# Second batch's attention in the paired form of the later batches, from step 10

## The chip, the cores and the metric

The kernel runs on one core of a Trainium2 chip. The metric is the device time of one execution in microseconds (us), as the median of several runs; beside it stands one profiled execution, from which every trace row here is taken. TensorE (PE in the rows, its weight loads PEld) multiplies matrices, VectorE (DVE), ScalarE (ACT) and GpSimd (POOL) work element by element, SyncE (SP) issues the transfers.

## The reference

Eight batches of causal attention with a window of 128 keys and a linear bias by head, and behind it, over all 4608 tokens, a two-layer network with the mish activation. Cut to what matters:

```python
# q, k, v: batch 8, heads 8, tokens 576, head size 64
scores = q @ k.T / 8 + slope[h] * -(i - j)       # where 0 <= i - j < 128, else -1e9
attn = softmax(scores);  attn_out = attn @ v
x = attn_out.transpose(0, 2, 1, 3).reshape(4608, 512)
h = x @ w_in                                     # 512 -> 2048
g = h * tanh(softplus(h))                        # mish
out = g @ w_out                                  # 2048 -> 512
```

## The kernel before

**Stages.** Tokens go through the network in chunks: chunk c holds the first 512 tokens of batch c (the last 64 of all batches make up a ninth chunk, kept in DRAM in the meantime). Every chunk has a first layer (tiles h, 192 matmuls of 128x512, then mish on ScalarE into g) and a second layer (tiles po, output products). Values are split into a high and a low part, so that each product is three matmuls (gg is g in its two parts, si and so are the weights in theirs). A second layer has 32 steps: 16 weight blocks, each with two banks po0 and po1 and six matmuls a step ("a group of six"); after eight blocks a half of the chunk is complete and its two banks are copied out (ob), the first by VectorE, the second by ScalarE, before the next half may write a bank again.

**Attention beside it.** While chunk c is in its second layer, the attention of batch c+1 is placed between its groups. Heads go in pairs p = 0..3; a pair has two halves of 256 queries (`unit(b, p, half)`, eight of them in a batch) and the last 64 queries (`last_unit(b, p)`). A unit's steps are: `scores` (TensorE, into bank s), `exps(0)` and `exps(1)` (VectorE adds the bias and takes the maximum, tt-reduce into pz; ScalarE takes the exponential and its sum sm), `fold` (adds the two parts of the wrapped window; for the second batch on GpSimd, later on VectorE), `scale` (by 1/sm; for the second batch GpSimd, later VectorE and ScalarE), `weights` (TensorE transposes pz into the score bank, VectorE copies back and multiplies by masks), `values` (TensorE, value products into bank o for the first half and into bank pt_pl for the second), `late_half` (the value products of 64 rows each, `late_values`) and `split_x` (the result in two parts as input of the next first layer). The last queries have their own tiles pz_pl, pt_pl and pf_pl; pt_pl is also the bank of the second half's values.

**What sets the order.** Each step has a time in units (lists `times` in `unit` and `last_unit`); `attention(b)` adds the unit's number and sorts; the loop over chunks maps a unit time s to a place among the 32 steps by `begin + (n - 2.1 - begin) / units * s` with n = 32 and sorts once more. TensorE's and SyncE's instructions then stay in that order. Those of VectorE, ScalarE and GpSimd are put in order when the program is built, except where `in_order` fixes them; each engine executes its own queue strictly in order.

**The second batch is special.** Chunk 0's second layer starts inside the hand-written opening (`FIRST_STEPS`), which does groups up to the fifth block and ends with the conversion of the weights; so only 22 of the 32 steps are left for the second batch's attention, where later batches have all 32. Before the change it has its own times: half 1's scores a unit after half 0's, the late products of half 0 apart from those of half 1, and `begin, units = 11.5, 9.0` with a `lead` for the first two units.

Of the kernel before, what the change touches and what calls it, by code (L numbers as in the profile page):

```python
# [68 lines left out]
def attention_mish_mlp(  # L69
# [85 lines left out]
    def load(dst, src):  # L155
        sp.dma_start(out=dst, in_=src)
# [140 lines left out]
    def load_pair(b, p):  # L297
        t = at.tile([P, QKZ], F32, tag="qk", name=f"qk{b}_{p}")
        load(t, qk_[b, p])
        qkv[(b, p)] = parts_of(t)  # L300

    def load_v(b, p):

        pl, tag = (xp, f"x{p}") if p < NP - 1 else (at, "v")
        t = pl.tile([P, 2, 4, P], F32, tag=tag, name=f"v{b}_{p}", bufs=1)
        load(t, v[b, p])
        if b:
            load(vb[p % 2], vl_[b, p])
        qkv[("v", b, p)] = ((t[:, 0], t[:, 1]), vb[p % 2])

    def score_banks(name):
        return ps.tile([P, 2, 512], F32, tag="s", name=f"s{name}", bufs=2)
# [27 lines left out]
    def late_values(b, p):  # L340
        parts = late.pop((b, p))
        for n in range(max(len(part) for part in parts)):
            for i in range(2):
                for part in parts:
                    if n < len(part):
                        o, val, w = part[n](i)
                        pe.matmul(o, lhsT=val, rhs=w, start=False, stop=n == len(part) - 1, skip_group_check=True)

    def unit(b, p, half):
# [122 lines left out]
                        part(b, p, o, 256 * u)  # L472

        def late_half():
            if b == 1 or half == 1:
                late_values(b, p)

        times = (0, 0.02, 0.25, 0.7, 0.95, 1.3, 1.99, 2.02, 1.9995)
        if b > 1:

            times = (
                (-1, -0.8, -0.7, -0.57, -0.25, 0.7 if p == 1 else 0.65, 0.97, 0.996, 0.995) if half
                else (0, 0.02, 0.12, 0.4, 0.45, 1.4 if p == 1 else 1.3, 1.96, 1.96, 1.96)
            )
        return list(zip(times, (
            scores, lambda: exps(0), lambda: exps(1), fold, scale, weights, values, split_x, late_half,
        )))

    def last_unit(b, p):

        st = {}
        name = f"{b}_{p}l"

        def scores():
            _, keys, z = qkv[(b, p)]

            t = qkv[("s", b, p)] = score_banks(f"{b}_{p}_0")
            st["s"] = t[:, :, :96]
            for a in range(2):
                for r in HEAD:  # L500
                    pe.matmul(
                        st["s"][r, a, :], lhsT=z[:, r], rhs=keys(slice(0, P), 384 + 96 * a, 96),
                        start=True, stop=True, skip_group_check=True,
                    )

        def exps():
            mx = at.tile([P, 1], F32, tag="mxl", name=f"mx{name}")
            sm = st["sm"] = at.tile([P, 1], F32, tag="sml", name=f"sm{name}")
            pz = st["pz"] = at.tile([P, 192], F32, tag="pzl", name=f"pz{name}")
            dve.tensor_tensor_reduce(  # L510
                out=pz.rearrange("p (a n) -> p a n", a=2), in0=st["s"],
                in1=nl[:, p, :].rearrange("p (a n) -> p a n", a=2), scale=-SCALE, scalar=3.0e38,
                op0=ALU.add, op1=ALU.min, accum_out=mx,
            )
            act.activation(pz, pz, AF.Exp, bias=mx, scale=-1.0, accum_out=sm)

        def fold():
            sm, pz = st["sm"], st["pz"]
            act.activation(sm, sm, AF.Copy, bias=1e-9)
            dve.reciprocal(sm, sm)  # L520
            un = at.tile([P, 1], F32, tag="unl", name=f"un{name}", bufs=1)
            dve.tensor_tensor_reduce(
                out=pz[:, :64], in0=pz[:, :64], in1=pz[:, P:], scale=sm, scalar=3.0e38,
                op0=ALU.add, op1=ALU.min, accum_out=un,
            )
            act.activation(pz[:, 64:P], pz[:, 64:P], AF.Copy, scale=sm)

        def weights():
            t = st["t"] = qkv[("t", b, p)] = ps.tile([P, 512], F32, tag="w", name=f"pt{name}")
            pe.transpose(t[:, :P], st["pz"][:, :P], ident)  # L530
            pf = st["pf"] = at.tile([P, 2, 2, 64], F32, tag="pfl", name=f"pf{name}", bufs=1)
            shape = [P, 2, 2, 64]
            dve.tensor_tensor(
                out=pf, in0=t[:, :P].rearrange("p (u i n) -> p u i n", u=1, i=2).to_broadcast(shape),
                in1=masks[:, :2, :64].rearrange("p u (i n) -> p u i n", i=1).to_broadcast(shape),
                op=ALU.mult,
            )

        def values():
            va, vl = qkv[("v", b, p)]  # L540
            o = st["o"] = qkv[("ol", b, p)][:, 256 : 256 + LEFT]
            for i in range(2):
                pe.matmul(
                    o[HEAD[i]], lhsT=va[0][:, 3, HEAD[i]], rhs=st["pf"][:, 0, i, :],
                    start=False, stop=False, skip_group_check=True,
                )
            late[(b, p)][0].append(lambda i: (o[HEAD[i]], vl[:, HEAD[i]], st["pf"][:64, 1, i, :]))

        def keep():
            o = st["o"]  # L550
            xo = at.tile([P, LEFT], F32, tag="xo", name=f"xo{name}", bufs=5)
            dve.tensor_copy(xo, o)
            sp.dma_start(out=xs[p, :, b * LEFT : (b + 1) * LEFT], in_=xo)

        times = (-0.001, 0.5, 0.9, 1.4, 1.995, 1.9996)
        if b > 1:
            times = (-0.035, 0.21, 0.44, 1.78 if p == 1 else 1.7, 1.98, 1.9955)
        return list(zip(times, (scores, exps, fold, weights, values, keep)))

    def first_attention():  # L560
# [181 lines left out]
    def attention(b):  # L742

        steps = []
        for k in range(2 * NP):
            p, half = divmod(k, 2)

            lead = (0.7, 0.35)[k] if b == 1 and k < 2 else 0
            work = unit(b, p, half)
            if b == 1 and k < 2:

                for n in ((3,), (1, 2))[k]:
                    work[n] = (work[n][0], lambda f=work[n][1]: in_order(f))
            steps += [(k + d - (lead if n < 5 else 0), f) for n, (d, f) in enumerate(work)]
            if half == 0:
                steps += [(k + d - (lead if n < 3 else 0), f) for n, (d, f) in enumerate(last_unit(b, p))]
            if half:  # L760
                nxt = (b, p + 2) if p + 2 < NP else (b + 1, p + 2 - NP)
                if 0 < nxt[0] < B:
                    steps.append((k + 0.03, lambda nxt=nxt: load_pair(*nxt)))
                if b and p < 2:
                    steps.append((k + (1.0 if b > 1 else 2.01), lambda p=p: load_v(b, p + 2)))
        return sorted(steps, key=lambda s: s[0])

    def last_x():
# [30 lines left out]
    def mish(c, j):  # L799
        f = 2 * (j % 2)  # L800
        act.activation(gt[(c, j // 2)][:, f : f + 2, :], hs.pop((c, j)), AF.Mish)
# [3 lines left out]
    def parts(c, half, j):  # L805
        parts_high(c, half, j)
        parts_low(c, half, j)
# [59 lines left out]
    def in_order(work):  # L867
        dve.fixed = act.fixed = True
        work()
        dve.fixed = act.fixed = False  # L870
# [29 lines left out]
    steps = first_attention()  # L900
# [30 lines left out]
    for c in range(B + 1):  # L931
        for j in range(NJ if c else 0):
            if j == NJ - 1:
                parts(c, 0, 0)
                parts(c, 0, 1)
            first(c, j)
            mish(c, j)

        n = 4 * NJ
        steps = []  # L940
        if 0 < c < B - 1:
            steps += [(-0.5, lambda p=p: load_v(c + 1, p)) for p in range(2)]
        for m in range(2 * NJ):
            if c or f"U{m}" not in done:
                for t in range(2):
                    steps.append((2 * m + t, lambda m=m, t=t: second(c, *divmod(m, NJ), t)))
            if m >= 2 and (c or f"R{m}" not in done):
                steps.append((2 * m - 4.1, lambda m=m: parts(c, *divmod(m, NJ))))
        if c + 1 < B:
            begin, units = (1.4, 8.0) if c else (11.5, 9.0)  # L950
            steps += [(begin + (n - 2.1 - begin) / units * s, f) for s, f in attention(c + 1)]
        elif c + 1 == B:
            steps.append((4.5, last_x))
        for _, work in sorted(steps, key=lambda s: s[0]):
            work()
# [85 lines left out]
```

## Time and profile before

| | us |
|---|---|
| median of 3 runs (965.27 to 966.36) | 966.11 |
| profiled execution | 965.23 |
| its span in the trace | 963.5 |
| TensorE busy | 955.9 |
| ScalarE busy | 459.5 |
| VectorE busy | 351.5 |
| GpSimd busy | 257.3 |

The profiled execution lasts 1.7 us longer than its span, which counts from the first to the last instruction. Busy is the union of an engine's instructions; since matmuls are pipelined, a busy TensorE still has a start-to-start distance that depends on what follows what, so stretches are compared from start to start here. "idle before, <-" in a row is the time in which the engine waited and the engine that ended it.

### The profile page before, as it was taken

The page shows a single profiled execution, that of the slowest core. Times are in us where ns is not written, and L with a number is a line of the kernel's source. Part 1 is how long each engine was busy: PE and PEld are TensorE (multiplying, and loading weights), DVE is VectorE, ACT ScalarE, POOL GpSimd, SP SyncE. Part 2 cuts the span into 40 slices and gives each one's busy share as a digit, 9 for nine tenths or more (in the row PEclk, how much of TensorE's full clock was granted, in tenths as well). Part 3 has the DMA queues.
Part 4 walks back from the last instruction along what each step waited for, and adds up shares of the span by engine and source line. Part 5 has one row for each costly group of instructions (what it writes and reads, how often), then busy time and mean ns, then how long its engine had stood idle before and what let it go on. Part 6 is the DMA issues. An engine that isn't in the chain of part 4 may idle for free.

```text
span 963.5 us, 17830 instructions
## 1 busy us (share of the span) xinstructions
PE 955.9 (99%) x6868; PEld 781.3 (81%) x6868; DVE 351.5 (36%) x1456; ACT 459.5 (48%) x1290; POOL 257.3 (27%) x228
## 2 busy tenths in 40 slices
PE   9999999999999999999999999999999999999998
PEld 7788778888888888888888888888888888888886
DVE  6998660067203650166204640166005730100000
ACT  7997642276425752376225742466316642322121
POOL 5588541022112221032102311032102311241042
PEclk9999999999999999999999999999999999999999
DMA  9962320123002310122002310222003110000001
GB/s 345 395 245 90 109 78 22 41 86 105 24 1 74 127 48 6 54 84 93 24 1 95 107 54 1 74 79 77 24 23 105 50 46 1 22 22 22 1 15 29
DMA packets 29636, 69.83 MB, mean 72 GB/s; under 512 B 7408, under 2 KB 9712, under 8 KB 29552
## 3 DMA queue, kind: packets, MB, share of 16 engines
q1 hardware_dynamic: 29552, 68.69, 20.6%
q8 instruction: 54, 0.88, 0.4%
q14 instruction: 30, 0.25, 0.1%
HBM read 58.20 MB, written 10.49 MB: 71 GB/s over the span
## 4 chain that ended last, share of the span: by engine, by line
PE 88%; DMA 5%; DVE 4%; ACT 2%; issue 1%; SPq 0%; DVEq 0%; ACTq 0%
PE po L57 39%; PE h L57 36%; PE s L57 7%; PE o L57 3%; DMA wi<-in_moe_w_in_dram 2%; DVE to L57 1%; DMA wo<-in_moe_w_out_dram 1%; DMA v<-in_v_dram 1%; DVE pz L57 1%; PE pt_3l L57 1%; PE pt_2l L57 1%; PE pt_1l L57 1%; PE pt_0l L57 1%; DMA first<-in_tabs_dram 0%; DVE wo L57 0%
## 5 line engine op out<-in xcount | busy, mean ns | idle before, releaser
L57 PE MATMUL po<-so,gg 128*128 128x512 f32 x1728 | 420.8, 396 | 0.0
L57 PE MATMUL h<-x,si 128*128 128x512 f32 x1728 | 393.8, 389 | 0.0
L57 PEld LDWEIGHTS h<-x,si 128*128 128x128 f32 x1728 | 324.1, 188 | 67.4
L57 PEld LDWEIGHTS po<-so,gg 128*128 128x128 f32 x1728 | 317.1, 188 | 71.7 <-issue 8.9
L57 POOL TENSOR_TENSOR gg<-g,gg 128x512 fp32r<-128x512 f32 x144 | 186.2, 1296 | 650.0 <-ACT gg L57 647.2
L57 ACT ACTIVATE g<-h 128x1024 f32<-128x1024 f32 x72 | 74.1, 1029 | 257.0 <-PE h L57 255.3
L57 DVE CUSTOM_DVE_ANT_0 pz<-s,nb 64x128 f32<-64x128 f32 (+1 forms) x280 | 83.1, 327 | 292.4 <-PE s L57 289.9
L57 ACT ACTIVATE pz<-pz,mx 128x192 f32<-128x192 f32 (+1 forms) x256 | 110.8, 434 | 39.0 <-DVE mx L57 37.0
L57 ACT ACTIVATE gg<-g 128x512 fp32r<-128x512 f32 x144 | 90.0, 625 | 69.6 <-PE po L57 67.3
L57 PE MATMUL s<-qk 64*64 64x192 f32 (+2 forms) x1120 | 56.6, 300 | 0.0
L57 DVE CUSTOM_DVE_ANT_0 pz<-pz,sm 128x64 f32<-128x64 f32 x144 | 55.9, 436 | 1.3
L57 DVE COPY ob<-po 128x512 f32<-128x512 f32 x10 | 6.9, 692 | 128.1 <-PE po L57 128.1
L57 ACT ACTIVATE pz<-pz,sm 128x128 f32<-128x128 f32 (+1 forms) x192 | 53.2, 347 | 0.1
L57 DVE TENSOR_TENSOR pz<-s,masks 128x512 f32<-128x512 f32 (+1 forms) x56 | 51.5, 945 | 2.6 <-PE s L57 2.6
L57 ACT ACTIVATION_READ_ACCUMULATOR pz<-pz,mx 128x1 f32 x256 | 47.8, 187 | 0.0
L57 PEld LDWEIGHTS s<-qk 64*64 64x64 f32 (+1 forms) x1120 | 42.5, 134 | 3.9 <-issue 2.8
L57 PE MATMUL s<-ident,pz 128*128 128x128 f32 (+1 forms) x280 | 42.9, 275 | 0.4 <-POOL pz L57 0.3
L57 PEld LDWEIGHTS o<-pz,v 128*64 128x64 f32 (+1 forms) x656 | 30.2, 135 | 15.5 <-DVE pz L57 5.4
L57 PEld LDWEIGHTS s<-ident,pz 128*128 128x128 f32 (+1 forms) x280 | 34.5, 138 | 10.1 <-POOL pz L57 1.1
L57 PE MATMUL o<-pz,v 64*64 64x64 f32 (+3 forms) x656 | 40.5, 250 | 0.4 <-DVE pz L57 0.4
L57 ACT ACTIVATE ob<-po 128x512 f32<-128x512 f32 x26 | 15.6, 599 | 44.1 <-PE po L57 44.1
L57 DVE DVE_READ_ACCUMULATOR2_ANT mx<- 128x1 f32 (+1 forms) x312 | 25.3, 81 | 0.0
(172 smaller groups left out, 551.8 us busy)
## 6 DMA issues: line engine op xcount, KB each, us to landing
qk<-in_qk_dram SPq DMA_DIRECT2D x28, 640.0 KB, 4.3
v<-in_v_dram SPq DMA_DIRECT2D x32, 512.0 KB, 4.3
wi<-in_moe_w_in_dram SPq DMA_DIRECT2D x16, 512.0 KB, 10.5
wo<-in_moe_w_out_dram SPq DMA_DIRECT2D x16, 512.0 KB, 10.2
out_dram<-ob SPq DMA_DIRECT2D x32, 256.0 KB, 2.0
first<-in_qk_dram SPq DMA_DIRECT2D x2, 848.0 KB, 9.6
xr<-xs SPq DMA_DIRECT2D x4, 256.0 KB, 2.7
out_dram<-ob SPq DMA_DIRECT2D x8, 128.0 KB, 2.4
```

Of the source, the lines that this page charges most:

```text
L57: ins = method(*args, **kwargs)
```

## The change

The second batch gets the times of the third and later batches: half 1's scores directly behind half 0's, weights of half 1 shortly behind those of half 0, late products of both halves together (`late_half` acts in half 1 alone). `lead` and the `in_order` marks of the first two units are gone, the loads of v come at unit time 1.0, and the attention begins at step 10 with 8 units over the rest. `fold` and `scale` stay on GpSimd for the second batch.

```diff
         def late_half():
-            if b == 1 or half == 1:
+            if half == 1:
                 late_values(b, p)
...
-        times = (0, 0.02, 0.25, 0.7, 0.95, 1.3, 1.99, 2.02, 1.9995)
-        if b > 1:
-
-            times = (
-                (-1, -0.8, -0.7, -0.57, -0.25, 0.7 if p == 1 else 0.65, 0.97, 0.996, 0.995) if half
-                else (0, 0.02, 0.12, 0.4, 0.45, 1.4 if p == 1 else 1.3, 1.96, 1.96, 1.96)
-            )
+        times = (
+            (-1, -0.8, -0.7, -0.57, -0.25, 0.7 if p == 1 else 0.65, 0.97, 0.996, 0.995) if half
+            else (0, 0.02, 0.12, 0.4, 0.45, 1.4 if p == 1 else 1.3, 1.96, 1.96, 1.96)
+        )
...
-        times = (-0.001, 0.5, 0.9, 1.4, 1.995, 1.9996)
-        if b > 1:
-            times = (-0.035, 0.21, 0.44, 1.78 if p == 1 else 1.7, 1.98, 1.9955)
+        times = (-0.035, 0.21, 0.44, 1.78 if p == 1 else 1.7, 1.98, 1.9955)
...
-            lead = (0.7, 0.35)[k] if b == 1 and k < 2 else 0
-            work = unit(b, p, half)
-            if b == 1 and k < 2:
-
-                for n in ((3,), (1, 2))[k]:
-                    work[n] = (work[n][0], lambda f=work[n][1]: in_order(f))
-            steps += [(k + d - (lead if n < 5 else 0), f) for n, (d, f) in enumerate(work)]
+            steps += [(k + d, f) for d, f in unit(b, p, half)]
...
-                    steps.append((k + (1.0 if b > 1 else 2.01), lambda p=p: load_v(b, p + 2)))
+                    steps.append((k + 1.0, lambda p=p: load_v(b, p + 2)))
...
-            begin, units = (1.4, 8.0) if c else (11.5, 9.0)
+            begin, units = (1.4, 8.0) if c else (10.0, 8.0)
```

How it moves instructions, at three places. Names carry batch, pair and half: s1_0_1 and pz1_0_1 are batch 1, pair 0, half 1; pt1_0l is the last queries' bank of pair 0; po0_0_1 is chunk 0, half 0, bank 1; an operand "ident" marks a transpose.

TensorE, first pair of the second batch, before: from the first half's transposes to the next pair's first scores.

```order
L57 MATMUL s1_0_0_1216<-ident_78,pz1_0_0_1231 128x128 x4
L57 MATMUL pt1_0l_1320<-ident_78,pz1_0l_1250 128x128
L57 MATMUL po0_0_1_1082<-so7_1068,gg0_0_7_1204 128x512 x6
L57 MATMUL o1_0_1333<-pz1_0_0_1231,v1_0_1069 64x192 x2
L57 MATMUL o1_0_1333<-pz1_0_0_1231,v1_0_1069 64x64 x2
L57 MATMUL o1_0_1333<-pf1_0l_1322,v1_0_1069 64x64 x2
L57 MATMUL s1_1_0_1340<-qk1_1_680 64x96 x4
```

TensorE, first pair, after: from the first half's transposes to the second half's values.

```order
L57 MATMUL s1_0_0_1210<-ident_78,pz1_0_0_1240 128x128 x4
L57 MATMUL po0_0_0_1075<-so7_1068,gg0_0_7_1204 128x512 x6
L57 MATMUL s1_0_1_1229<-ident_78,pz1_0_1_1253 128x128 x4
L57 MATMUL pt1_0l_1326<-ident_78,pz1_0l_1260 128x128
L57 MATMUL o1_0_1330<-pz1_0_0_1240,v1_0_1069 64x192 x2
L57 MATMUL o1_0_1330<-pz1_0_0_1240,v1_0_1069 64x64 x2
L57 MATMUL s1_1_0_1335<-qk1_1_680 64x96 x4
L57 MATMUL pt1_0l_1326<-pz1_0_1_1253,v1_0_1069 64x64 x8
```

Both halves' transposes now stand with one group between them, and no group stands between the second half's transposes and the value products.

ScalarE around the output copy ob of chunk 0's first half, before: the copy stands ahead of the second pair's exponentials (pz1_1 with two operands).

```order
L57 ACTIVATE sm1_0_1_1281<-sm1_0_1_1281 128x4
L57 ACTIVATE ob0_0_1308<-po0_0_1_1082 128x512
L57 ACTIVATE gg0_1_2_1371<-g0_1_803 128x512
L57 ACTIVATE pz1_1_0_1364,sm1_1_0_1363<-pz1_1_0_1364,mx1_1_0_1362 128x128 x2
L57 ACTIVATE pz1_1_0_1364,sm1_1_0_1363<-pz1_1_0_1364,mx1_1_0_1362 128x192 x2
```

ScalarE, after: from the second pair's first exponentials to the copy.

```order
L57 ACTIVATE pz1_1_0_1402,sm1_1_0_1401<-pz1_1_0_1402,mx1_1_0_1400 128x128 x2
L57 ACTIVATE pz1_1_0_1402,sm1_1_0_1401<-pz1_1_0_1402,mx1_1_0_1400 128x192 x2
L57 ACTIVATE pz1_1_1_1415,sm1_1_1_1414<-pz1_1_1_1415,mx1_1_1_1413 128x192
L57 ACTIVATE sm1_1_0_1401<-sm1_1_0_1401 128x4
L57 ACTIVATE pz1_1_1_1415,sm1_1_1_1414<-pz1_1_1_1415,mx1_1_1_1413 128x192
L57 ACTIVATE pz1_1l_1422,sm1_1l_1421<-pz1_1l_1422,mx1_1l_1420 128x192
L57 ACTIVATE pz1_1_1_1415,sm1_1_1_1414<-pz1_1_1_1415,mx1_1_1_1413 128x192 x2
L57 ACTIVATE ob0_0_1318<-po0_0_1_1082 128x512
```

The copy has moved behind all nine exponentials of the second pair.

GpSimd in the first pair, before: low parts of gg, folds (two operands alike) and scales (with sm).

```order
L57 TENSOR_TENSOR gg0_1_0_1256<-g0_0_683,gg0_1_0_1256 128x512
L57 TENSOR_TENSOR pz1_0_0_1231<-pz1_0_0_1231 128x2x64
L57 TENSOR_TENSOR pz1_0_0_1231<-pz1_0_0_1231,sm1_0_0_1230 128x4x128
L57 TENSOR_TENSOR pz1_0_1_1282<-pz1_0_1_1282 128x4x64
L57 TENSOR_TENSOR gg0_1_1_1299<-g0_0_683,gg0_1_1_1299 128x512
L57 TENSOR_TENSOR pz1_0_1_1282<-pz1_0_1_1282,sm1_0_1_1281 128x4x128
```

GpSimd in the first pair, after.

```order
L57 TENSOR_TENSOR pz1_0_0_1240<-pz1_0_0_1240 128x2x64
L57 TENSOR_TENSOR pz1_0_0_1240<-pz1_0_0_1240,sm1_0_0_1239 128x4x128
L57 TENSOR_TENSOR pz1_0_1_1253<-pz1_0_1_1253 128x4x64
L57 TENSOR_TENSOR gg0_1_0_1286<-g0_0_683,gg0_1_0_1286 128x512
L57 TENSOR_TENSOR pz1_0_1_1253<-pz1_0_1_1253,sm1_0_1_1252 128x4x128
```

The first low part of gg has moved from ahead of the first half's fold to between the second half's fold and its scale.

## Rows read from the trace of the kernel before

**Rows 1.** The page: busy time (share, instructions) by engine; last chain by engine.

```profile
PE 955.9 (99%) x6868; PEld 781.3 (81%) x6868; DVE 351.5 (36%) x1456; ACT 459.5 (48%) x1290; POOL 257.3 (27%) x228
...
PE 88%; DMA 5%; DVE 4%; ACT 2%; issue 1%; SPq 0%; DVEq 0%; ACTq 0%
```

**Rows 2.** TensorE's waits, whole span, two of five: us in total, times, longest.

```profile
PE warm L57 <- DVE first L57: 1.1, 1, 1.1
...
PE o L57 <- DVE pz L57: 0.4, 1, 0.4
...
```

**Rows 3.** Output products po alone: stretch, its length, busy (count) by engine, granted clock.

```profile
94.27:146.47 52.20, 33.73 (x127) 22.29 (x126) 1.38 (x2) 0.60 (x1) 1.00 0.26 86
189.99:252.79 62.80, 47.24 (x192) 34.88 (x191) 0.69 (x1) 1.20 (x2) 1.00 0.27 87
```

**Rows 4.** The same view for h: a whole first layer of 192 matmuls.

```profile
252.95:296.47 43.52, 43.52 (x192) 35.69 (x191) 7.20 (x7) 1.00 0.06 19
```

**Rows 5.** One pair, second and third batch: length, PE PEld DVE ACT POOL, clock.

```profile
106.62:117.67 11.05, 11.00 (x133) 8.42 (x129) 8.10 (x34) 6.79 (x26) 5.76 (x7) 1.00 0.35 116
208.76:222.98 14.22, 14.22 (x149) 11.65 (x147) 9.47 (x47) 10.58 (x38) 5.24 (x4) 1.00 0.36 126
```

**Rows 6.** Timeline of TensorE, third batch, first pair: start, duration, what.

```profile
201.93 1.63 PE L57 MATMUL po<-so,gg 128*128 128x512 f32 x6
203.40 0.60 PE L57 MATMUL s<-ident,pz 128*128 128x128 f32 x4
...
203.86 1.64 PE L57 MATMUL po<-so,gg 128*128 128x512 f32 x6
205.44 0.66 PE L57 MATMUL o<-pz,v 128*64 128x192 f32 x8
205.93 0.50 PE L57 MATMUL s<-qk 128*64 128x96 f32 x8
206.26 0.64 PE L57 MATMUL pt_0l<-pz,v 128*64 128x64 f32 x16
```

**Rows 7.** Timeline of TensorE, second batch, first pair: the two score visits.

```profile
94.27 1.25 PE L57 MATMUL s<-qk 128*64 128x96 f32 x24
...
98.40 0.88 PE L57 MATMUL s<-qk 64*64 64x192 f32 x16
```

**Rows 8.** Timeline of the other engines, second batch, first half of the first pair.

```profile
95.97 0.28 DVE L57 CUSTOM_DVE_ANT_0 pz<-s,nb 64x128 f32<-64x128 f32 x1
...
96.61 0.40 ACT L57 ACTIVATE pz<-pz,mx 128x128 f32<-128x128 f32 x1 [1.66 <-DVE mx L57]
...
98.09 0.61 ACT L57 ACTIVATE gg<-g 128x512 fp32r<-128x512 f32 x1
...
100.57 1.04 POOL L57 TENSOR_TENSOR pz<-pz,sm 128x512 f32<-128x512 f32 x1
```

**Rows 9.** Timeline of ScalarE, third batch, first pair: first and last of nine exponentials.

```profile
194.94 0.40 ACT L57 ACTIVATE pz<-pz,mx 128x128 f32<-128x128 f32 x1
...
198.55 0.44 ACT L57 ACTIVATE pz<-pz,mx 128x192 f32<-128x192 f32 x1
```

**Rows 10.** Timeline of GpSimd, second batch, second half of the first pair.

```profile
102.83 0.74 POOL L57 TENSOR_TENSOR pz<-pz 128x256 f32<-128x256 f32 x1 [1.23 <-ACT pz L57]
103.53 1.28 POOL L57 TENSOR_TENSOR gg<-g,gg 128x512 fp32r<-128x512 f32 x1
...
104.77 1.04 POOL L57 TENSOR_TENSOR pz<-pz,sm 128x512 f32<-128x512 f32 x1
```

**Rows 11.** Timeline, second batch: output copy, last queries' mask, second half's mask.

```profile
104.20 0.60 ACT L57 ACTIVATE ob<-po 128x512 f32<-128x512 f32 x1 [0.83 <-PE po L57]
104.41 0.41 DVE L57 TENSOR_TENSOR pf_0l<-pt_0l,masks 128x256 f32<-128x256 f32 x1
...
108.89 1.22 DVE L57 TENSOR_TENSOR pz<-s,masks 128x1024 f32<-128x1024 f32 x1
```

**Rows 12.** The page's DMA issues: KB each, median us from issue to landing.

```profile
qk<-in_qk_dram SPq DMA_DIRECT2D x28, 640.0 KB, 4.3
```

More of the change, by code (lines that the diff above doesn't have):

```diff
@@ L749, in attention @@
             p, half = divmod(k, 2)
-            lead = (0.7, 0.35)[k] if b == 1 and k < 2 else 0
-            work = unit(b, p, half)
-            if b == 1 and k < 2:
-                for n in ((3,), (1, 2))[k]:
-                    work[n] = (work[n][0], lambda f=work[n][1]: in_order(f))
-            steps += [(k + d - (lead if n < 5 else 0), f) for n, (d, f) in enumerate(work)]
+            steps += [(k + d, f) for d, f in unit(b, p, half)]
             if half == 0:
-                steps += [(k + d - (lead if n < 3 else 0), f) for n, (d, f) in enumerate(last_unit(b, p))]
+                steps += [(k + d, f) for d, f in last_unit(b, p)]
             if half:
```

## The prediction

> **What bounds the kernel now.** I read the page first: TensorE is busy for 955.9 us of 963.5, and the chain that ended last is 88% TensorE [rows 1]. Then its waits: over the whole span TensorE waits for another engine five times, never longer than 1.1 us, and in the stretch that the change touches once, 0.4 us for a VectorE mask [rows 2]. So a microsecond of TensorE work taken away is a microsecond of time, and a microsecond of new waiting is lost in full; the other engines count only where TensorE waits for them.
>
> The stretch is that of the second batch's attention, 94.27 to 146.47 us: 52.20 us, with 126 output products (one weight load each, so I count them by the loads) [rows 3]. A product costs 0.2267 us where nothing is between: 192 matmuls of that shape take 43.52 us [rows 4]. So the attention costs TensorE 52.20 - 126 x 0.2267 = 23.64 us there, 0.4 of them that wait. The third batch, already in the form that the second now takes, has 62.80 - 192 x 0.2267 = 19.28 us [rows 3]. By pairs of heads: 11.05 us with 24 products (5.61 left) against 14.22 us with 42 (4.70 left) [rows 5].
>
> **The change part by part.** *TensorE's own work.* The late value products of the two halves run side by side, scores of both halves are one visit, and there are fewer changes between products and attention. The third batch shows 23.24 - 19.28 = 3.96 us less. It has three runs of products in a pair, the second batch four before; by the new order it has two now. One change more that falls away is worth the surplus of a lone run of six: 1.47 and 1.58 us from start to start [rows 6] against 6 x 0.2267 = 1.36, so 0.11 to 0.22 us, about 0.6 for four pairs. I take 4.6 us, from 4.0 to 5.0. The old wait of 0.4 goes too: 5.0 in all.
>
> *New waits.* The third batch pays for this form with cover: between scores and values it has 42 products a pair. The second has 22 groups of six in all, and about 30 products a pair even with the earlier start. The new order puts three groups (the first pair) or four (the others; the second needs one of them otherwise, see below) between the scores and the first half's transposes, one group between those and the second half's, and none between these and the values. I lay the other engines' work end to end against that.
>
> First pair. TensorE's score visits of 1.25 and 0.88 us [rows 7] now stand together, but for the last queries' scores, which go one group ahead. So its three groups run from about 96.2 to 100.4. VectorE takes the first scores at 95.97, as before: until then it converts weights. In the old order GpSimd had the first half scaled at 100.57 + 1.04 = 101.6, with a 0.61 us copy of gg among its exponentials [rows 8]; without that copy it is 100.6 to 101.0. **Wait 0.4** (0.2 to 0.6). The second half's exponentials now follow directly: the third batch does its nine and a sum in 198.55 + 0.44 - 194.94 = 4.05 us [rows 9]. From 96.61 that ends at 100.7. Then GpSimd folds (0.74), does a low part of gg that is queued between (1.28) and scales (1.04) [rows 10]: 103.8, 103.9 with the handovers. TensorE is there 0.35 + 1.47 after it resumed [rows 6], at 102.5. **Wait 1.5** (1.0 to 1.9).
>
> Masks. After the second half's transposes VectorE needs 1.22 for their mask and 0.41 for that of the last queries [rows 11], which follow each other; the value products write the bank that the second reads. With handovers 1.75 us. Before the first product that needs them TensorE has the first half's value products and the next pair's last scores, 206.26 - 205.44 = 0.82 us in the third batch [rows 6], and the tail of a transpose, some 0.15. In the third batch a run of six lies ahead of these; here nothing does. **Wait 0.75** in three pairs, **1.1** in the last, which has no next scores: 3.4 (2.4 to 4.2).
>
> Second pair. The output copy ob of the first half's second bank (0.60 us [rows 11]) has moved on ScalarE from ahead of the second pair's exponentials to behind all nine. The third product group after the visit writes that bank's successor, so TensorE waits for the copy, and behind it in TensorE's queue stand the rest of the stage. ScalarE starts 0.64 us after VectorE's first score read [rows 8], takes 4.05, then 0.60: 5.3 us after the visit's end. TensorE has two groups, 2.8. **Wait 2.6** (2.2 to 3.0). This hides the second pair's transposes, since GpSimd is done meanwhile.
>
> Third and fourth pairs. The second half is scaled 0.64 + 4.05 + 0.74 + 1.28 + 1.04 = 7.75 us after the visit, 7.9 with handovers; TensorE is there after 4 x 1.37 + 0.35 + 1.47 = 7.3. **Wait 0.5** each (0 to 0.8).
>
> Sum of new waits 0.4 + 1.5 + 3.4 + 2.6 + 1.0 = 8.9 us (6.5 to 10.7).
>
> *Moved at no cost.* Loads of v go out earlier. The queries and keys of the fourth pair are now queued on SP behind the output that waits for the late copy; 4.3 us from issue to landing [rows 12] lie beside a whole pair of 11 us, and would cost 4.3 if that cover were gone. The split of x for both halves together is due only in the next layer. Later batches keep their order, so what the stage loses is not given back.
>
> *A rule against the change.* In the stretches shown the granted clock is 1.00, which is 2.4 GHz [rows 3 to 5], and TensorE never idled for over 1.1 us [rows 2]; here it would for 2.6. The Trainium skill, in TensorE: Matmul & The Clock Gate, Part 1 (The HAM clock gate), says that the clock falls to half after the engine idled and comes back only when it has been busy again. No row of this trace shows 1.2 GHz, so it doesn't enter the sum; it is a rival below.
>
> **The sum.** 8.9 - 5.0 = +3.9 us. Handing over from engine to engine, which I rounded down in places, lets me take **+4.1**. On the profiled execution (965.23 us, 1.7 of them around the span) this is 969.3; the runs' median is 0.9 higher, at 966.11, so **970.2 us**. From the ends: waits 6.5 less gains of 5.4 and waits 10.7 less gains of 4.4 are +1.1 and +6.3; both ends together are unlikely, but handovers push upward, so I take +1.9 to +6.9: 968.0 to 973.0.
>
> **The rivals.** *All covered: faster.* TensorE finds its operands ready as in the third batch, whose visits have the same form: there TensorE is busy for all 14.22 us of a pair [rows 5]. Then the 5.0 us stay: 961.1. It decides at waits of 5.0 in sum. For it: the same helper code, and shares of VectorE and ScalarE of 73% and 61% in a pair before [rows 5], so there is room on average. Against it: the wait is on a chain, not on a share, and the cover is 30 products instead of 42. Chance 0.05.
>
> *Half covered: no change.* The mask waits vanish (if the products that follow need only a mask that is done early) and so do those of the third and fourth pairs; 0.4 + 1.5 + 2.6 = 4.5 remain against 5.0: 965.6. Against it: no product run stands between transposes and values. Chance 0.08.
>
> *The clock falls.* A wait of 2.6 us, or several close together in the first two pairs, lets the granted clock fall to 1.2 GHz; a group of six then takes 2.72 instead of 1.36. If one or two groups run so, 1.4 to 2.7 us come on top, and if a whole pair's work of 11 us does, 11: 972 to 981. For it: nothing before idles that long. Against it: the waits are singular, with full product runs between. Chance 0.05, and by the page's rule it would be one of the longer waits that sets it off.
>
> *It doesn't do what it says* can be left out: the new order shows the paired visits in all four pairs.
>
> **Chances.** My forecast 0.82, all covered 0.05, half covered 0.08, clock 0.05. About 0.2% (1.9 us) is what a measurement of this kernel can tell from no change. Faster 0.05; same 0.08; slower 0.87. The range of 968.0 to 973.0 leaves out the faster and the unchanged case, most of the clock's, and little of the forecast.
>
> **What would show it.** In the profile after, TensorE's first matmul of the second batch's first layer starts about 4 us later than at 146.47, and all batches after are shifted by the same. TensorE's waits list three new kinds: for GpSimd's pz ahead of transposes (about 3 us in sum), for VectorE's pf ahead of value products (four times, 3.4), for ScalarE's ob once (2.6). Without its waits the stage is some 4.6 us shorter. Wrong would be: no wait for ob (then ScalarE's order doesn't bind, and the loss falls to 1.5), waits for GpSimd of several us in all pairs (the chain is longer than laid out), a granted clock under 1.00 in the stretch, or a difference that arises in later batches.

## The result and the profile after

| | before | after |
|---|---|---|
| median of 4 runs, us | 965.69 (965.25 to 966.36) | 972.11 (971.78 to 973.61) |
| ratio, 95% interval | | 1.0070 (1.0058 to 1.0083) |
| profiled execution, its span | 965.23, 963.5 | 972.02, 970.3 |

The change makes the kernel 6.4 us slower. Six of TensorE's ten kinds of waits after, over the whole span (us in total, times, longest), where before there were those of [rows 2]:

```profile
PE s L57 <- POOL pz L57: 2.8, 5, 1.4
PE po L57 <- ACT ob L57: 2.5, 1, 2.5
...
PE pt_3l L57 <- DVE pf_3l L57: 1.0, 1, 1.0
PE pt_0l L57 <- DVE pf_0l L57: 0.7, 1, 0.7
PE pt_1l L57 <- DVE pf_1l L57: 0.7, 1, 0.7
PE pt_2l L57 <- DVE pf_2l L57: 0.7, 1, 0.7
...
```

All three new kinds are there: GpSimd's scaled pz (three of the five, 2.06 us; the other two lie in the opening, at 9.79 and 28.02), VectorE's mask pf in each pair, ScalarE's copy ob once. To see what else moved, I measure one stretch in every kernel, from the first output product of chunk 0's second layer to the second batch's first h. The two ends in the timeline of TensorE (start, duration, what), of before and then of after:

```profile
79.22 15.12 PE L57 MATMUL po<-so,gg 128*128 128x512 f32 x66
...
146.47 13.76 PE L57 MATMUL h<-x,si 128*128 128x512 f32 x60
```

```profile
79.45 13.76 PE L57 MATMUL po<-so,gg 128*128 128x512 f32 x60
...
153.25 6.96 PE L57 MATMUL h<-x,si 128*128 128x512 f32 x30
```

Before it is 67.25 us, after 73.80: 6.55 more. The first h comes 6.78 later (0.23 of it stood ahead of the stretch already), and the span is longer by as much (963.5 to 970.3). So in sum nothing is given back later, and nothing added. The waits in it (the bracket: idle before, and what ended it) can be read singly; three of the eight:

```profile
104.30 0.66 PE L57 MATMUL s<-ident,pz 128*128 128x128 f32 x4 [1.37 <-POOL pz L57]
...
106.67 0.69 PE L57 MATMUL pt_0l<-pz,v 128*64 128x64 f32 x16 [0.69 <-DVE pf_0l L57]
...
114.71 4.60 PE L57 MATMUL po<-so,gg 128*128 128x512 f32 x12 [2.47 <-ACT ob L57]
```

The eight are 1.37, 0.69, 2.47, 0.69, 0.49, 0.69, 0.20 and 1.02 us, 7.62 in sum, against 0.38 before. The last of these rows shows a second thing: twelve products take 4.60 us there, where a group of six takes 1.36 from start to start. By the stretches of the second pair (length, PE PEld DVE ACT POOL, granted clock) and of what follows that wait:

```profile
109.22:125.85 16.63, 13.47 (x138) 10.59 (x136) 8.13 (x35) 7.64 (x28) 7.05 (x7) 0.90 0.29 93
...
115.00:118.30 3.30, 3.30 (x9) 2.52 (x9) 1.32 (x4) 1.34 (x5) 2.39 (x3) 0.50 0.81 266
```

The granted clock is 0.50, that is 1.2 GHz, right behind the wait of 2.47 us; its record lasts 3.41 us (114.96 to 118.38), in which TensorE is busy throughout, so at half the clock it costs half of that, 1.71. The rest follows by subtraction: 6.55 = 7.24 (waits) + 1.71 (clock) - 2.40 (TensorE's own work). I had given the own work 4.6.

### The profile page after: what moved, and what is told of

The parts are those of the page before. It is cut to its first block, busy times and chain, and to the rows that moved or that the text cites. A ratio compares the mean times of both kernels' runs of the same rounds, so it can differ in the third digit from the quotient of the medians.

```text
span 970.3 us, 17833 instructions
## 1 busy us (share of the span) xinstructions
PE 955.1 (98%) x6868; PEld 781.9 (81%) x6868; DVE 350.8 (36%) x1456; ACT 458.6 (47%) x1290; POOL 257.2 (27%) x228
## 4 chain that ended last, share of the span: by engine, by line
PE 86%; DMA 6%; DVE 3%; ACT 2%; issue 1%; POOL 1%; SPq 0%; DVEq 0%; ACTq 0%; POOLq 0%
PE po L57 38%; PE h L57 36%; PE s L57 7%; PE o L57 3%; DMA wo<-in_moe_w_out_dram 2%; DMA wi<-in_moe_w_in_dram 2%; DVE to L57 1%; ACT pz L57 1%; DVE pz L57 1%; DMA first<-in_qk_dram 1%; PE pt_3l L57 1%; PE pt_0l L57 1%; PE pt_2l L57 1%; PE pt_1l L57 1%; POOL pz L57 1%
```

## The experiments

The same reading of all kernels. "Own" is the stretch without its waits and without what the clock cost: 1.71 for each fall inside it, but 1.42 for the first one of e_gap, of whose 3.41 us 0.58 lie in the wait itself. The median and the ratio are of all runs of a kernel, the ratio to the kernel before as measured beside it (medians 965.23 to 965.73); stretch, waits and falls are of the one profiled execution.

| kernel | median, us | ratio to before, 95% | stretch | waits (number) | falls | own |
|---|---|---|---|---|---|---|
| before | 965.69 | | 67.25 | 0.38 (1) | 0 | 66.87 |
| after | 972.11 | 1.0058 to 1.0083 | 73.80 | 7.62 (8) | 1 | 64.47 |
| e_ob | 970.03 | 1.0029 to 1.0059 | 72.49 | 6.43 (8) | 1 | 64.35 |
| e_undolate | 972.13 | 1.0051 to 1.0081 | 72.43 | 5.92 (8) | 0 | 66.51 |
| e_late | 976.30 | 1.0091 to 1.0125 | 76.45 | 9.07 (4) | 1 | 65.67 |
| e_begin | 969.29 | 1.0021 to 1.0043 | 69.60 | 2.48 (1) | 0 | 67.12 |
| e_gap | 973.50 | 1.0065 to 1.0095 | 75.97 | 8.94 (4) | 2 | 63.90 |
| e_spread | 967.45 | 1.0010 to 1.0029 | 69.02 | 4.83 (7) | 0 | 64.19 |
| e_half1 | 970.06 | 1.0022 to 1.0050 | 70.20 | 6.09 (7) | 0 | 64.11 |
| e_short | 968.00 | 1.0014 to 1.0032 | 69.42 | 4.77 (9) | 0 | 64.65 |
| e_behind | 964.67 | 0.9985 to 1.0002 | 66.03 | 2.57 (4) | 0 | 63.46 |
| e_split | 964.24 | 0.9980 to 0.9999 | 66.04 | 1.87 (8) | 0 | 64.17 |

In runs without a profile a fall is read from the mean granted clock: every run of the kernel before had 0.999 or 1.000, the profiled executions with falls inside 0.995 to 0.998. A single 0.998 is no sure sign: one run of e_split has it, whose waits in the profile are 0.29 us at most.

### Parts taken out of the change

**e_ob: the copy ob by VectorE** instead of ScalarE, for chunk 0's first half.

```diff
-            if t == 0 and (half or c == 0):
+            if t == 0 and (half or c == 0) or c == half == 0:
```

> The changed kernel with one thing different: the second bank of chunk 0's first half is copied out by VectorE, not by ScalarE. Theory (the loss is waits of TensorE, plus the clock that falls after the longest of them): the wait of 2.47 us for ScalarE's copy becomes one of about 1.3 us for VectorE's, the granted clock stays at 1.00 in the stretch, a little waiting for GpSimd (0.3 us) comes back in the second pair; 2.5 us faster than the changed kernel, about 969.5 us. Rival (the paired visits cost TensorE more work of their own, and that wait and the clock are incidental): no change, 971.5 to 972.5 us.

Measured 970.03. The wait for ScalarE is gone, and one of 0.92 us for VectorE's copy stands in its place; the other waits stay. The clock did not stay at 1.00: in the profiled run it fell at 146.68, behind the last pair's waits of 0.55 and 1.02 us (143.93 and 146.31). The other three runs have a mean clock of 0.999 or 1.000, where each of the four after has 0.997 or 0.998. So the medians give ob 2.1 us (2.5 expected), in part by the clock; taking the longest wait away made the fall rarer, but didn't rule it out.

**e_undolate: the late products of the two halves apart**, as before.

```diff
-            if half == 1:
+            if b == 1 or half == 1:
                 late_values(b, p)
```

> The changed kernel with the late value products of the two halves apart again (the first half's right behind its own products). Theory: the waits stay, those for VectorE's masks some 0.3 us shorter each because more lies ahead of them; TensorE's own work grows by 0.4 us a pair; the wait for the copy and the fall of the clock stay: 971 to 973 us. Rival (the paired late products are what costs): 966 to 968.5 us.

Measured 972.13, no gain and no loss. The profiled run had no fall of the clock, although the wait for ob is there; the other three have a mean clock of 0.997 or 0.998. TensorE's waits:

```profile
PE po L57 <- ACT ob L57: 2.4, 1, 2.4
...
PE pt_3l L57 <- DVE pf_3l L57: 0.6, 1, 0.6
...
PE pt_2l L57 <- DVE pf_2l L57: 0.2, 1, 0.2
PE pt_0l L57 <- DVE pf_0l L57: 0.2, 1, 0.2
PE pt_1l L57 <- DVE pf_1l L57: 0.2, 1, 0.2
```

The waits for masks shrink by 0.53 in three pairs and 0.38 in the last, because the first half's late products now lie ahead of them, and the own work grows by 2.0 (64.47 to 66.51). What the pairing of the late products saves was therefore paid back at the masks almost in full (1.97 us), since nothing else stands there.

### Parts of the change alone

**e_late: the late products together, in the kernel before** (`if half == 1` in `late_half`). In it the last queries' part of the output lacks the late products, which come behind its copy.

> The kernel before with one part of the change alone: the second batch's late value products of both halves stand together; times and begin stay as before. Theory: the first half's weights pz are then read a unit later, and pz has two buffers, so that the next pair's exponentials wait for the buffer and TensorE for them: three waits of about 3.3 us, 974.5 us, and up to 980 if the clock falls after each. Rival (the paired late products are a plain saving that the waits elsewhere ate): no new waits, 0.4 us less a pair, about 964.5 us.

Measured 976.30. TensorE's timeline:

```profile
116.11 0.67 PE L57 MATMUL s<-ident,pz 128*128 128x128 f32 x4 [2.89 <-POOL pz L57]
...
131.43 0.66 PE L57 MATMUL s<-ident,pz 128*128 128x128 f32 x4 [2.91 <-POOL pz L57]
...
145.21 0.66 PE L57 MATMUL s<-ident,pz 128*128 128x128 f32 x4 [2.91 <-POOL pz L57]
```

Three times 2.9 us (3.3 expected), in every pair that has one ahead of it, and a mean clock of 0.995 to 0.998 in the four runs. The next pair's first write of pz on VectorE waits for TensorE's value products into o, the late ones among them from 110.28 on:

```profile
110.79 0.28 DVE L57 CUSTOM_DVE_ANT_0 pz<-s,nb 64x128 f32<-64x128 f32 x1 [1.18 <-PE o L57]
```

A pz that is kept for the late products blocks one of its two buffers, so the next pair's exponentials start later. With two buffers of pz, as here, late products together go with scores together.

**e_begin: the early start alone, in the kernel before.**

```diff
-            begin, units = (1.4, 8.0) if c else (11.5, 9.0)
+            begin, units = (1.4, 8.0) if c else (10.0, 9.0)
```

> The kernel before with the start alone moved: the second batch's attention begins at step 10 instead of 11.5 with 9.0 units, all visits and late products as before. If an earlier start alone gave cover for the chain, the time would be 965.5 or less. By the order laid out with the durations of before: TensorE comes to the first pair's transposes about 2.9 us ahead of GpSimd's scaling, since the first scores, held by VectorE's weight conversions, don't come earlier by as much; elsewhere waits don't change. So +2.9 us and 0.2 for the wait, 968.6, and 970.3 if the clock falls after it.

Measured 969.29, with 2.48 us at the place expected:

```profile
101.91 0.66 PE L57 MATMUL s<-ident,pz 128*128 128x128 f32 x4 [2.48 <-POOL pz L57]
```

The scores stand 1.4 us earlier (92.84 against 94.27 [rows 7]), but VectorE still reads the first at 95.89 (95.97 before, [rows 8]). The start moved the demand, not the supply. Three of the seven runs have a mean granted clock of 0.997, and 969.4 to 969.6 us; of the four at 0.999, three have 967.6 to 967.8 (the fourth, 969.29, is the median). So a fall shows in whole runs too, with some 1.8 us; both levels lie some 0.9 us below the 968.6 and 970.3 expected.

### Cover moved

**e_gap: one group between the second half's transposes and the values.**

```diff
+        if b == 1 and half:
+            times = times[:5] + (0.5,) + times[6:]
```

> The changed kernel with one group of six placed between the second half's transposes and the value products of each pair of the second batch (the weights of half 1 at 0.5 instead of 0.65 and 0.7). If the four waits for VectorE's masks (0.69, 0.69, 0.69, 1.02 us) come from the missing cover there, they vanish. The group is taken from ahead of the second half's transposes, so the waits for GpSimd there grow to 2.9, 2.0 and 1.9 us in three pairs by the durations of the trace; the wait for the output copy stays. Theory (the chain from scores to values is longer than the products of a pair, so cover can only be moved): no gain, 972 to 974. Rival (order of the visits is what is wrong, the cover is enough): waits 3.1 us less, about 969.

Measured 973.50. All waits of its stretch in TensorE's timeline:

```profile
103.85 1.11 PE L57 MATMUL s<-ident,pz 128*128 128x128 f32 x4 [2.72 <-POOL pz L57]
116.36 4.63 PE L57 MATMUL po<-so,gg 128*128 128x512 f32 x12 [2.48 <-ACT ob L57]
134.68 0.65 PE L57 MATMUL s<-ident,pz 128*128 128x128 f32 x4 [1.87 <-POOL pz L57]
148.15 0.66 PE L57 MATMUL s<-ident,pz 128*128 128x128 f32 x4 [1.87 <-POOL pz L57]
```

The mask waits are gone, and GpSimd's have grown from 2.06 to 6.46: the cover was only moved, as the theory had it. The clock fell at 103.27, in the first of the two longest waits, and at 116.92, behind the other; not with those of 1.87. All four runs have a mean clock of 0.998 or less.

**e_spread: the fold on VectorE, and the start at 10.15 with 7.9 units.** This shortens the chain by a piece and spreads the products so that the copy ob is in time.

```diff
-                pool.tensor_tensor(out=two[:, :, both], in0=two[:, :, :64], ...
+                dve.tensor_tensor(out=two[:, :, both], in0=two[:, :, :64], ...
...
-            begin, units = (1.4, 8.0) if c else (10.0, 8.0)
+            begin, units = (1.4, 8.0) if c else (10.15, 7.9)
```

> The changed kernel with the second batch's attention from step 10.15 in 7.9 units (so that the output copy of the first half stands ahead of the visit, and one group of products between the second half's transposes and the values) and the fold of the second batch on VectorE. Theory: no wait for ScalarE's copy, none of over 1.2 us, clock at 1.00; the waits are spread (about 0.9 us, eight times, 7 us in sum), since the chain from scores to values is longer than its cover: 968 us, slower than before by 2 to 3 us. Rival (the loss comes from the bad places of two waits alone): waits of under 2 us in sum, about 963.5 us.

Measured 967.45. No wait for ob or a mask, seven for GpSimd, 4.83 us in sum where 7 were expected. The two edits were made together, and no run tells what each brought. What stood in the chain is seen in GpSimd's timeline of the third pair:

```profile
127.92 1.29 POOL L57 TENSOR_TENSOR gg<-g,gg 128x512 fp32r<-128x512 f32 x1 [0.76 <-ACT gg L57]
129.16 1.04 POOL L57 TENSOR_TENSOR pz<-pz,sm 128x512 f32<-128x512 f32 x1
```

A low part of gg, not due yet, is done ahead of the scaling for which TensorE idles 0.99 us (at 130.25).

### What one wait costs

The kernel before, with GpSimd delayed once ahead of the fifth batch's first layer, in which TensorE otherwise never waits (e_w5 and e_w6: five and six passes):

```diff
+    zero = const.tile([P, 1], F32, tag="zero", name="zero")
+    nc.gpsimd.memset(zero, 0.0)
...
+                if b == 4 and p == 3:
+                    low = xt[(b, p)][:, 1, :]
+                    for _ in range(5):
+                        pool.tensor_tensor(out=low, in0=low.bitcast(F32), in1=zero.to_broadcast([P, CH]), op=ALU.subtract)
```

> The kernel before, in which GpSimd subtracts zero from the low part of the fifth batch's last input tile five times more, 1.04 us each. That puts one wait of TensorE into a first layer that has none: laid out with the durations of the trace of before, 1.55 us at the eleventh h matmul, around 468 us. Theory 1 (a wait costs its length and some 0.2 us of lost overlap with it): the layer of 192 matmuls, 43.52 us before, takes 43.52 + 1.55 + 0.2 = 45.3 us, the run 1.75 us more than before, about 967.3. Rival (a wait costs its length alone): 45.1 us from first to last matmul. Clock: 1.00 if only waits of some 2.5 us or several in a row lower it; a fall to 0.5 here would say that a wait of 1.5 us is enough.

> The same with six passes: one wait of 2.6 us, as long as the wait for the output copy in the changed kernel (2.47 us), but single and in a stretch with no other wait. Theory 1 (a wait of this length by itself lowers the clock): granted clock 0.5 for 3.41 us after it, so 2.6 + 0.2 + 1.7 = 4.5 us, about 970.0, in all or some of the runs. Rival (it takes several waits near each other): clock 1.00, 2.8 us, about 968.4.

Measured 967.89 and 970.08 (ratios 1.0012 to 1.0030 and 1.0025 to 1.0059). TensorE in that layer, from its first h to the product behind it, before, with five and with six passes:

```profile
465.63 43.68 PE L57 MATMUL h<-x,si 128*128 128x512 f32 x192
509.15 2.88 PE L57 MATMUL po<-so,gg 128*128 128x512 f32 x12
```

```profile
466.92 2.43 PE L57 MATMUL h<-x,si 128*128 128x512 f32 x10
470.99 41.55 PE L57 MATMUL h<-x,si 128*128 128x512 f32 x182 [1.65 <-POOL x L57]
512.38 2.88 PE L57 MATMUL po<-so,gg 128*128 128x512 f32 x12
```

```profile
465.91 2.43 PE L57 MATMUL h<-x,si 128*128 128x512 f32 x10
471.10 43.14 PE L57 MATMUL h<-x,si 128*128 128x512 f32 x182 [2.76 <-POOL x L57]
514.08 2.20 PE L57 MATMUL po<-so,gg 128*128 128x512 f32 x9
```

43.52 us, 45.46 and 48.17. A wait of 1.65 made the layer 1.94 longer: 0.29 more than itself. One of 2.76 made it 4.65 longer: 1.71 of it is the clock, which fell at 471.87 for 3.41 us, and 0.18 remain. The stretch behind that wait (length, PE PEld DVE ACT POOL, granted clock):

```profile
471.10:475.30 4.20, 4.20 (x11) 3.34 (x12) 0.00 (x0) 0.00 (x0) 0.00 (x0) 0.59 0.00 0
```

So theory 1 holds in both profiled runs: a wait costs some 0.2 to 0.3 us besides the length that the trace shows, and a single wait of 2.8 us can lower the clock by itself. It does so not always: two of the four runs with six passes have a mean clock of 0.997 (970.25 and 970.59), two have 0.999 or more (969.92 and 969.22). With five passes all ten runs have 0.999 or 1.000. Since the ends of matmuls are modelled in a profile, the runs don't tell whether the 0.2 to 0.3 us are lost overlap or a part of the wait that the trace doesn't show.

### A shorter chain

**e_half1: the second half's scaling on VectorE**, and **e_short: both halves', with the offset of sm**, on top of the version with the fold on VectorE.

```diff
-                pool.tensor_tensor(
+                (dve if half else pool).tensor_tensor(
                     out=pz[:, :, folded], in0=pz[:, :, folded],
```

> The changed kernel with the fold on VectorE and the start at 10.15 with 7.9 units (967.45 us, waits for GpSimd's scaling 5.4 us in nine), and besides the second half's scaling of the second batch on VectorE as one multiplication of 128x512 (some 0.7 us by VectorE's copies and sums of that size, against 1.04 on GpSimd, where it also stood behind a low part of gg of 1.29). Theory (the length of the chain from scores to values is what the paired form lacks, so each step taken off it comes back as time): the second half's waits of some 1.0 each fall to 0.4, laid out 2.5 us less than with GpSimd, some 965.0 us, about as the kernel before. Rival (the first half's chain and VectorE's queue behind the multiplication take it back): 967 to 968.

> The same with both halves' scaling on VectorE, and the sum's small offset (1e-9) added by VectorE instead of ScalarE, where it can stand behind a 0.62 us part of gg. That is the shortest chain that could be laid out: waits 0.2 to 0.7 each, 4 us in sum at most, 2.6 us less than with GpSimd. Theory: 964 to 965.5, at or just under the kernel before. Rival (VectorE's queue becomes the chain: multiplications of half 0 stand among the reads of half 1's scores): 966.5 to 968.

Measured 970.06 and 968.00: neither theory. The second is at the upper end of its rival, the first is 2 us beyond its own: in three of its five runs the mean clock is 0.997 (970.06 to 970.36 us), the two others have 968.64 and 968.77. And the reason isn't the one given for either rival. VectorE's two multiplications of the third pair in the second kernel, and beside them GpSimd:

```profile
127.39 0.69 DVE L57 TENSOR_TENSOR pz<-pz,sm 128x512 f32<-128x512 f32 x1
...
129.21 1.67 DVE L57 TENSOR_TENSOR pz<-pz,sm 128x512 f32<-128x512 f32 x1
```

```profile
129.03 2.98 POOL L57 TENSOR_TENSOR gg<-g,gg 128x512 fp32r<-128x512 f32 x2 [9.71 <-ACT gg L57]
```

The same multiplication takes 0.69 us while GpSimd is idle and 1.67 while it works, and GpSimd's two take 2.98 instead of the 2.53 that they take in e_split (below). In both kernels together the six that stand beside GpSimd take 1.56 to 1.76, the six others 0.69; in e_half1 GpSimd's two are not delayed (2.51 and 2.52). So the step didn't get shorter than the 1.04 it replaced. The Trainium skill, SBUF — State Buffer, "SBUF: two separate sides", says that VectorE with two inputs in SBUF and GpSimd take turns for a whole instruction. The rows agree: GpSimd's first gg would end at 130.3, and VectorE's multiplication ends at 130.88, some 0.6 us behind that.

**e_behind: the low part of gg behind the scaling.** GpSimd's order is written out for this layer, both scalings are on GpSimd again, the offset of sm stays on VectorE. The second kernel (e_split) also gives the first half's scaling to VectorE, at a time when GpSimd is idle.

```diff
-                steps.append((2 * m - 4.1, lambda m=m: parts(c, *divmod(m, NJ))))
+                steps.append((2 * m - 4.1, lambda m=m: (parts if c else parts_high)(c, *divmod(m, NJ))))
+                if c == 0:
+                    steps.append((2 * m - 3.9, lambda m=m: parts_low(c, *divmod(m, NJ))))
...
+        pool.fixed = c == 0
```

> The kernel with the fold on VectorE and the start at 10.15 (967.45 us; its three middle waits ahead of the second half's transposes, 1.0 to 1.1 each, stand behind a low part of gg of 1.29 us that GpSimd does ahead of the scaling), with GpSimd's order written out so that the low part of gg comes behind the second half's scaling, and the sum's offset added by VectorE instead of ScalarE. Both scalings stay on GpSimd, so VectorE multiplies nothing beside it. Theory (the length of the chain is what the form lacks, and the low part of gg was in it): the waits ahead of the second half's transposes go, those ahead of the first half's stay at 0.5 to 0.7; laid out 2.0 us less, some 965.3, level with the kernel before. Rival (the products now wait for a low part of gg that comes too late, or VectorE's masks become late): 967 or more.

> The same, with the first half's scaling on VectorE (0.69 us alone there, since GpSimd has nothing to do at that time) and the second half's on GpSimd (1.04). By the order laid out the sum of the waits is the same as with both on GpSimd, since the second half's transposes end the chain; it only moves from the first half's (0.3 each) to the second half's (0.5 each): 965.3 again. If it is over 0.7 us better or worse than the former, the sum of waits doesn't hang on the second half alone.

Measured 964.67 and 964.24. GpSimd in the third pair of the second kernel, and TensorE's two waits there:

```profile
126.48 1.11 POOL L57 TENSOR_TENSOR pz<-pz,sm 128x512 f32<-128x512 f32 x1 [8.77 <-DVE sm_2l L57]
127.55 2.53 POOL L57 TENSOR_TENSOR gg<-g,gg 128x512 fp32r<-128x512 f32 x2
```

```profile
125.36 0.63 PE L57 MATMUL s<-ident,pz 128*128 128x128 f32 x4 [0.29 <-DVE pz L57]
...
127.64 0.66 PE L57 MATMUL s<-ident,pz 128*128 128x128 f32 x4 [0.25 <-POOL pz L57]
```

The scaling now comes first, and eight waits make 1.87 us. In the first kernel none is left ahead of the second half's transposes (1.0 to 1.1 each in e_spread); how much of this is GpSimd's order and how much the moved offset was not tried apart. The first of the two kernels is level with the kernel before, the second is 0.1% faster, with an interval (0.9980 to 0.9999) that just leaves 1 out; among a dozen kernels that is no proof of a gain. Between the two the stretch is the same (66.03, 66.04), with four waits of 2.57 or eight of 1.87: what the shorter waits give, their number takes. So the loss of the paired form goes away once the chain behind it is short enough; that it gains is not shown. The change as made left the chain as it was.

## Why the prediction was right, and where it was not

**Right:** that it gets slower, by new waits that outweigh TensorE's saved work, with the time inside the range (972.1 in 968.0 to 973.0); the three kinds of wait and their places; that later batches give nothing back.

**The waits, term by term.** First pair's second half: 1.5 taken, 1.37 measured. Masks: 0.75 in three pairs and 1.1 in the last, measured 0.69 three times and 1.02. The copy ob: 2.6, measured 2.47. Third and fourth pairs' second halves: 0.5 each, measured 0.49 and 0.20. The first pair's first half: 0.4, not there; GpSimd had it scaled at 99.78 + 1.04 = 100.82, and the transposes started at 100.88. In sum 7.62 instead of 8.9.

**The bounds of the waits** were mis-added: the ends of the single terms make 5.8 and 11.3 us, not 6.5 and 10.7, and I gave no reason for the narrower pair.

**TensorE's own work was mis-sized:** 4.6 us taken (4.0 to 5.0), 2.40 measured. I took the surplus of the third batch, which has no waits, as that of the second with eight. But each wait adds something besides its length. The five kernels that start at 10.15 have the same order on TensorE, and their own work grows with the number of waits: 63.46 with four, 64.11 and 64.19 with seven, 64.17 with eight, 64.65 with nine. The three that start at 10.0 with paired late products have 63.90 with four, 64.35 and 64.47 with eight. That is 0.13 to 0.24 us a wait ((64.41 - 63.90) / 4 and (64.65 - 63.46) / 5), and the delayed first layers gave 0.18 and 0.29 for one. Eight of them are 1.0 to 1.9 us. Taken back to none, the change stands at 62.6 to 63.4 against 66.7 before: 3.3 to 4.1 us saved, at or under the low end of what I took. That is an estimate, no kernel here had the form without waits.

**The clock** was a rival with a chance of 0.05, at 1.4 to 2.7 us for one or two groups. It came true, beside the forecast and not instead of it: 1.71 us in the profiled run, and the mean granted clock was 0.997 or 0.998 in each of the four runs after. My reason against it, that the waits stand singly with full products between, fell with the delayed first layer, where one wait of 2.76 was enough. The Trainium skill, TensorE: Matmul & The Clock Gate, Part 1 (The HAM clock gate), has the rule that the clock halves after the engine idled and comes back after it was busy. The rows agree where the clock fell behind a wait of 2.47 us and was back at 118.38; that the length of a wait alone doesn't decide it is shown by two of 2.91, behind which it stayed at 1.00. Which wait sets it off is not settled. In the profiled runs 2.47, 2.72 and 2.76 did, the second of e_gap's (2.48), and the first of e_late's three (2.89), but not the two of 2.91 behind it; 2.44 and 2.48 in e_undolate and e_begin did not; the fall in e_ob stood behind 0.55 and 1.02; the waits between 0.99 and 1.93 in e_w5, e_spread, e_gap and e_half1 went without. But three of the five runs of e_half1, whose longest waits in the profiled run are 1.93 and 1.84, have a mean clock of 0.997, and one of the ten of e_spread has 0.998 (969.58 us): waits under 2 us seem able to do it too, which no profiled run shows, where one of 1.65 in e_w5 did not in ten runs.

**The sum.** Against the forecast the waits are 1.3 lower, the own work saves 2.2 less, and the clock adds 1.7: 2.6 more than the 3.9 summed, that is +6.5, and the stretch shows +6.55. That the time stayed in the range was luck in part: its upper end was left open for handovers, and what filled it was the clock, which the sum had at nothing, and the smaller saving.

**The other rivals** fell. All covered: each pair waited. Half covered: the mask waits were there in full, and a group moved between transposes and values removes them (e_gap, e_spread), in e_gap at the price of longer waits elsewhere.

## What to carry to other kernels

A form that saves work on the bounding engine by putting its visits together also makes the other engines' part one longer chain; lay that chain against the products that lie beside it before counting the saving, and price each new wait with its length, some 0.2 us more, and from about 2 us on the chance of a lowered clock. If the chain is too long, look first for work in it that isn't due (here a low part of gg ahead of a scaling); moving cover from one wait to another brought nothing here. A step given to a second engine is only shorter if the two don't get in each other's way.

## What the runs showed of the hardware

- With a wait of 2.5 to 2.9 us TensorE's granted clock fell to 0.5 for 3.41 us, in some executions and not in others of the same kernel (e_w6: two of four, e_begin: three of seven); with waits of up to 1.93 us its mean was lower in three of five (e_half1).
- Single waits of TensorE, with 128x512 products on both sides, cost 0.18 and 0.29 us besides their shown length (e_w6, e_w5).
- VectorE's multiplication of 128x512 with both operands in SBUF takes 0.69 us alone and 1.56 to 1.76 beside GpSimd's subtractions (e_half1, e_short), and delays these in some places (2.98 for two, against 2.53) but not in all (2.52).
